# A fused attention and two-MLP kernel: the second head mix in calls of 128 keys, the scores in calls of up to 120 rows

## The chip, the cores and the metric

One core of a Trainium2 chip. The metric is the device time of one execution in microseconds (us); lower is better. The kernel before takes 1315.55 us, the median of three runs (1312.03 to 1316.77).

## The reference

Talking-heads attention feeds a gated MLP, and that a second MLP. All is float32; batch 4, 12 heads, 448 rows and keys, head size 64.

```python
scores = scale * np.matmul(q, k.transpose(0, 1, 3, 2))
scores = np.einsum('bhij,hg->bgij', scores, w_pre)        # first mix over heads
scores = scores - np.max(scores, axis=-1, keepdims=True)
attn = np.exp(scores)
attn = attn / (np.sum(attn, axis=-1, keepdims=True) + 1e-09)
attn = np.einsum('bhij,hg->bgij', attn, w_post)           # second mix over heads
x = np.matmul(attn, v)                                    # then 1792 x 768
x = (1 / (1 + np.exp(-(x @ w_gate))) * (x @ w_val)) @ w_out   # 768 -> 1536 -> 768
h = np.maximum(x @ w_in, 0.0)                             # 768 -> 2048
out = h * h @ w_out2
```

## The kernel before

Attention comes first, then the two MLPs. The query rows of a batch are cut into tiles of 60 to 120 rows, 17 tiles in all. A tile is cut into groups of 10 rows, and two groups make a duo; there are 90 duos. An iteration of the main loop puts out, in program order, the work of several duos at several stages. On TensorE the order within an iteration is: the first mix of duo t (`premix`), the scores of a later tile for one pair of heads when the list `front` says so (`scores`), the second mix of a duo three iterations back (`postmix`), and every few iterations a product with the values (`values`).

- `scores` (L190 to L220) takes one pair of heads of one tile. For each head of the pair (`o`), 64 rows of the array hold the head's q and 448 keys stream through. Up to 64 query rows are taken per call (the loop over `c0`, L203), so a tile of 100 rows takes two calls, of 64 and 36 columns. ScalarE copies both PSUM banks to SBUF (`e`, L214), and a DMA on SP's queue scatters them into `g` (L217), with heads and rows of a group together on the partitions.
- `premix` (L225) multiplies `g` by a block-diagonal matrix `wp` in four calls on 64 rows and 64 columns of the array each (L232), into `ps_m`. VectorE takes the maximum (L244), ScalarE the exponential (L251), VectorE the reciprocal of the sum (L259, L260), and GpSimd scales the second mix's weights by it (`wn`, L264).
- `postmix` (L273) has the exponentials `a` as the stationary operand: 60 rows (5 query rows by 12 heads) by a run of 64 keys. It streams the 60 columns of `wn`. A duo has two groups (`y`), two halves of the array's rows (`u`) and seven runs of 64 keys, so 28 calls (L289), each in a quarter of the array: `u` picks the rows and `o` the columns. The result stands with the keys on the partitions, in two PSUM banks; VectorE copies them to `ap` (L317).
- `values` (L327) multiplies `ap` by `v` over four blocks of 128 keys; 448 keys are three and a half blocks, and `v` is padded with zeros. Its calls use 128 rows and 64 columns of the array (L336).
- The four banks `bank` are lent in turn to scores, second mix and values by `room` (L394). They are cleared once at the start (L127), since the last half block of the second mix is never written.

In the innermost part of `postmix` a call's place in the array is set by the partitions it reads and writes:

```python
for o in range(min(2, -(-(S - jt * P) // HP))):
    j = min(jt * P + o * HP, S - HP)
    nc.tensor.matmul(ps[u][o * HP : (o + 1) * HP, y, jt], lhsT=x[r, j : j + HP], ...)
```

Beside this, `feed` puts out work for the MLPs as a planner with fixed costs says (`Feed`, L517): during attention it rearranges the weights (ScalarE L787 and L790, VectorE, GpSimd L807, DMAs on SP's queue), and after it the MLPs' 4284 matmuls (L917) follow in order. It steps by a fixed model time per iteration.

A float32 matmul call shows as two records in the trace, each with a weight load of its own (PEld). 2520 calls at L289 are 5040 records.

Of the kernel before, what the change touches and what calls it, by code (L numbers as in the profile page):

```python
# [19 lines left out]
P = 128  # L20
# [8 lines left out]
HP = P // 2  # L29
# [35 lines left out]
def attention(tc, feed, q, k, v, w_pre, w_post, xs, B, H, S, D):  # L65
# [10 lines left out]
    nc = tc.nc  # L76
# [24 lines left out]
    with ExitStack() as ctx, ExitStack() as mid, ExitStack() as left:  # L101
# [21 lines left out]
        g_of = [pg.tile([P, GT, S], F32, name=f"g{m}") for m in range(GB)]  # L123

        bank = [ps_b.tile([P, 4 * P], F32, name=f"ps_b{m}") for m in range(4)]
        for x in bank:
            nc.vector.memset(x, 0.0)  # L127

        def masks():
            nc.gpsimd.memset(wr, 0.0)  # L130
# [42 lines left out]
        k_t, q_t = {}, {}  # L173
# [16 lines left out]
        def scores(n, p):  # L190

            b, i0, rows = tiles[n]
            isz = full[n]
            if p == 0:
                g_t[n] = g_of[n % GB]
            kt = k_t.pop((b, p)) if i0 + rows == S else k_t[b, p]
            if n == 0 and p // 2 == 1:
                ps = [ps_m.tile([P, S], F32, tag="m", name="ps_s") for _ in range(2)]
            else:
                ps = [x[:, :S] for x in room(2)]  # L200
            for o in range(2):
                r = slice(o * D, (o + 1) * D)
                for c0 in range(0, isz, HP):  # L203
                    c = slice(c0, min(c0 + HP, isz))
                    nc.tensor.matmul(  # L205
                        ps[o][c], lhsT=q_t[n][r, p, c], rhs=kt[r], start=True, stop=True
                    )
            t = p4.tile([IM, 2, S], F32, tag="e", name="e")
            e = [t[:, o] for o in range(2)]
            for o in range(2):  # L210
                if o and n == 0:
                    nc.vector.tensor_copy(e[o][:isz], ps[o][:isz])
                else:
                    nc.scalar.copy(e[o][:isz], ps[o][:isz])  # L214
                to = g_t[n][G0 : G0 + GI * H].rearrange("(r h) g j -> h r g j", h=H)
                queue = nc.scalar if n == 0 and o else nc.sync
                queue.dma_start(  # L217
                    out=to[2 * p + o, :, : isz // GI],
                    in_=e[o][:isz],
                )  # L220
# [52 lines left out]
        def postmix(d):  # L273
            n, r0 = groups[duos[d][0]][:2]
            if r0 == 0:
                ap[n] = pp.tile([P, JT, H, IM], F32, tag="ap", name="ap")
            a, wn = a_t.pop(d)
            at = room(2)
            ps = [
                x[:, : 2 * JT * KH].rearrange("p (y t h r) -> p y t h r", y=2, t=JT, r=HB) for x in at  # L280
            ]

            for y, x in enumerate(a):
                for jt in range(JT):
                    for u in range(2):
                        r = slice(u * HP, u * HP + KH)
                        for o in range(min(2, -(-(S - jt * P) // HP))):
                            j = min(jt * P + o * HP, S - HP)
                            nc.tensor.matmul(  # L289
                                ps[u][o * HP : (o + 1) * HP, y, jt],  # L290
                                lhsT=x[r, j : j + HP],
                                rhs=wn[r, y].rearrange("p g i -> p (g i)"),
                                start=True,
                                stop=True,
                            )
            for u in range(2):
                pending.append((mixed, d, u, ps[u], at[u]))

# [81 lines left out]
        def next_scores():  # L380

            _, n, p = front.popleft()
            scores(n, p)
            if tiles[n][1] + tiles[n][2] == S:
                freed[0] += 1
            if p == (EARLY if n == 1 else 0) and n + 1 < NT:
                q_load(n + 1)
# [6 lines left out]
        def room(n):  # L394
            at = [bank.pop(0) for _ in range(n)]
            bank.extend(at)
            if any(x[-1] is y for x in pending for y in at):
                flush()
            return at
# [7 lines left out]
        for p in range(NP):  # L407
            scores(0, p)
        mixers()
        for _ in range(EARLY):  # L410
            scores(*front.popleft()[1:])
        for t in range(ND + 30):
# [18 lines left out]
            while done < ND and (done <= t - LAG or t >= ND and done <= t - 2):  # L431
                r0 = groups[duos[done][0]][1]
                n = groups[duos[done][0]][0]
                while r0 == 0 and todo and todo[0][1] <= n - 2:
                    values(*todo.popleft()[1:])
                    left_over -= VW
                postmix(done)
                left_over -= PW
                done += 1
                if done == ND or groups[duos[done][0]][0] != n:  # L440
                    todo.extend((t, n, h) for h in range(H // HV))
                if done == ND:
                    flush()
                    mid.close()
                    feed.widen(1)
# [714 lines left out]
@with_exitstack  # L1160
def whole(ctx, tc, q, k, v, w_pre, w_post, wg, wv, wo, wi2, wo2, out):
    B, H, S, D = k.shape[0], 2 * k.shape[1], k.shape[3], k.shape[2] // 2
    DM = out.shape[0]
    dram = ctx.enter_context(tc.tile_pool(name="dram", bufs=1, space=DRAM))
    xs = [dram.tile([DM, S], F32, name=f"xs{b}") for b in range(B)]
    with tc.manual_schedule():
        feed = mlp(ctx, tc, xs, wg, wv, wo, wi2, wo2, out)
        attention(tc, feed, q, k, v, w_pre, w_post, xs, B, H, S, D)
        feed.finish()
# [49 lines left out]
```

## Time and profile before

| | |
|---|---|
| median of three runs | 1315.55 us |
| profiled execution: time | 1321.79 us |
| profiled execution: span, first to last instruction | 1320.0 us |
| TensorE (PE) busy | 1233.4 us, 93% |
| weight loads (PEld) busy | 1062.1 us, 80% |
| VectorE / ScalarE / GpSimd busy | 77% / 61% / 23% |
| attention ends, MLP matmuls without a break begin | about 445 us |
| TensorE's granted clock, mean | 0.98 |

The profile gives each engine's busy time, the idle time before each group of instructions and what ended it. A record of a matmul lasts from its start to the modelled end of its pipeline, so records overlap, and the busy time of a group is the union of its records. "60*64 60x60" means a stationary operand of 60 rows by 64 columns, and 60 columns streamed.

### The profile page before, as it was taken

How to read it: one execution, taken by the hardware profiler on the slowest of the kernel's cores; microseconds unless marked ns; L12 is line 12 of the kernel's file. 1: busy time of each engine (PE TensorE's matmuls, PEld its weight loads, DVE VectorE, ACT ScalarE, POOL GpSimd, SP SyncE). 2: the span in 40 equal slices, each digit the busy share in tenths (PEclk: the TensorE clock that was granted, in tenths of full speed). 3: DMA queues.
4: the chain of work that ended last, by engine and by line, in shares of the span. 5: the costliest groups of instructions: out<-in, count | busy, mean ns of one | idle time of the engine just before them, and what ended most of it. 6: DMA issues, size and time to landing. Idle time of an engine off the chain costs nothing.

```text
span 1320.0 us, 32039 instructions
## 1 busy us (share of the span) xinstructions
PE 1233.4 (93%) x12476; PEld 1062.1 (80%) x12476; DVE 1020.6 (77%) x1681; ACT 805.5 (61%) x1545; POOL 307.8 (23%) x361
## 2 busy tenths in 40 slices
PE   5888978978887999999999999999999999999998
PEld 2556656655665999999999999998988999999998
DVE  3667667757776888899988789998899986566864
ACT  4676756756656756676666667665555675435553
POOL 5223333323332053420034343022342000000000
PEclk8999999989999999999999999999999999999999
DMA  5888888778787579874698887368686355334343
GB/s 171 227 222 239 232 247 238 230 235 236 224 242 252 158 261 313 294 259 133 201 311 287 295 297 224 115 217 313 207 281 212 108 179 170 108 108 110 108 130 108
DMA packets 151507, 280.50 MB, mean 213 GB/s; under 512 B 32892, under 2 KB 100796, under 8 KB 151356
## 3 DMA queue, kind: packets, MB, share of 16 engines
q1 hardware_dynamic: 150676, 277.81, 69.0%
q8 instruction: 98, 1.61, 0.5%
q10 hardware_dynamic: 680, 0.66, 0.2%
q14 instruction: 53, 0.43, 0.1%
HBM read 175.53 MB, written 63.31 MB: 181 GB/s over the span
## 4 chain that ended last, share of the span: by engine, by line
PE 74%; DMA 13%; DVE 6%; issue 3%; ACT 2%; SPq 0%; POOL 0%; ACTq 0%; DVEq 0%
PE ps L917 60%; DMA g<-e 4%; PE ps_b L336 4%; PE ps_b L289 4%; PE ps_m L232 3%; PE ps_b L205 3%; DMA raw<-in_wv 2%; DMA raw<-in_wo 2%; DMA raw<-in_wg 1%; DMA q<-in_q 1%; ACT a L251 1%; DVE ap L317 1%; DVE w L905 1%; DVE y L823 1%; DMA gv<-y 1%
## 5 line engine op out<-in xcount | busy, mean ns | idle before, releaser
L917 PE MATMUL ps<-s,w 128*128 128x448 f32 x4284 | 873.1, 366 | 7.6 <-DVE w L905 5.4
L917 PEld LDWEIGHTS ps<-s,w 128*128 128x128 f32 x4284 | 806.7, 188 | 73.9 <-DVE w L905 7.2
L905 DVE TENSOR_TENSOR w<-w,w 128x768 fp32r<-128x768 f32 x238 | 245.4, 1031 | 103.4 <-ACT w L902 101.5
L902 ACT CAST w<-w 128x768 fp32r<-128x768 f32 x238 | 199.1, 837 | 161.6 <-PE ps L917 135.1
L807 POOL TENSOR_TENSOR y<-y,raw 128x384 int32<-128x384 int32 x136 | 174.9, 1305 | 421.0 <-DVE y L796 177.4
L289 PEld LDWEIGHTS ps_b<-wn,a 60*64 60x64 f32 x5040 | 114.9, 138 | 54.8 <-issue 31.2
L317 DVE COPY ap<-ps_b 128x480 f32<-128x480 f32 (+2 forms) x177 | 108.3, 652 | 58.9 <-PE ps_b L289 58.7
L244 DVE TENSOR_REDUCE nm<-ps_m 128x1 f32<-128x448 f32 x180 | 103.4, 614 | 54.0 <-PE ps_m L232 53.9
L902 ACT CAST s<-g 128x448 fp32r<-128x448 f32 x196 | 109.8, 566 | 46.9 <-PE ps L917 38.8
L289 PE MATMUL ps_b<-wn,a 60*64 60x60 f32 x5040 | 119.9, 226 | 18.6 <-issue 11.5
L214 ACT COPY e<-ps_b 120x448 f32<-120x448 f32 (+2 forms) x196 | 95.0, 544 | 66.8 <-PE ps_b L205 48.7
L264 POOL TENSOR_SCALAR wn<-wq,sm 128x60 f32<-128x60 f32 x167 | 70.1, 435 | 261.7 <-DVE sm L260 198.0
L205 PE MATMUL ps_b<-k,q 64*64 64x448 f32 (+3 forms) x784 | 111.4, 578 | 19.2 <-DMA q<-in_q 8.7
L232 PE MATMUL ps_m<-g,wp 64*64 64x448 f32 (+1 forms) x720 | 104.9, 587 | 24.5 <-DMA g<-e 13.8
L905 DVE TENSOR_TENSOR s<-g,s 128x448 fp32r<-128x448 f32 x196 | 121.3, 633 | 3.2 <-ACT s L902 0.6
L251 ACT ACTIVATE a<-ps_m,nm 128x448 f32<-128x448 f32 x180 | 114.3, 648 | 13.6 <-PE ps_b L289 6.9
L336 PEld LDWEIGHTS ps_b<-ap,vraw 128*64 128x64 f32 x1632 | 76.8, 139 | 25.3 <-ACT e L214 14.5
L336 PE MATMUL ps_b<-ap,vraw 128*64 128x100 f32 (+4 forms) x1632 | 84.8, 261 | 12.9 <-ACT e L214 11.5
L205 PEld LDWEIGHTS ps_b<-k,q 64*64 64x64 f32 (+3 forms) x784 | 45.1, 135 | 61.8 <-issue 39.2
L787 ACT ACTIVATE raw<-raw 128x768 f32<-128x768 f32 x68 | 62.4, 918 | 39.7 <-DMA raw<-in_wo 11.0
L950 ACT COPY ps<-ps 128x448 f32<-128x448 f32 x104 | 52.0, 515 | 28.8 <-PE ps L917 28.1
L942 DVE TENSOR_TENSOR c<-ps,c 128x448 f32<-128x448 f32 x104 | 63.2, 619 | 7.7 <-PE ps L917 6.9
(49 smaller groups left out, 804.4 us busy)
## 6 DMA issues: line engine op xcount, KB each, us to landing
w<-wo SPq DMA_DIRECT2D x98, 384.0 KB
w<-gv SPq DMA_DIRECT2D x84, 384.0 KB
g<-e SPq DMA_DIRECT2D x108, 210.0 KB
raw<-in_wo SPq DMA_DIRECT2D x56, 384.0 KB
w<-wi SPq DMA_DIRECT2D x56, 384.0 KB
wo<-y SPq DMA_DIRECT2D x42, 384.0 KB
g<-e SPq DMA_DIRECT2D x84, 175.0 KB
gv<-y SPq DMA_DIRECT2D x36, 384.0 KB
```

The lines of the kernel that those rows point to most:

```text
L205: nc.tensor.matmul(ps[o][c], lhsT=q_t[n][r, p, c], rhs=kt[r], start=True, stop=True)
L214: nc.scalar.copy(e[o][:isz], ps[o][:isz])
L232: nc.tensor.matmul(ps[u * HP : (u + 1) * HP], lhsT=wp[r], rhs=g_t[n][r, 2 * t + u], start=True, stop=True,)
L244: nc.vector.tensor_reduce(out=nm[-1], in_=ps, op=ALU.max, axis=AX.X, negate=True)
L251: nc.scalar.activation(a, ps, AF.Exp, bias=nm, accum_out=sm[:, y : y + 1])
L289: nc.tensor.matmul(ps[u][o * HP : (o + 1) * HP, y, jt], lhsT=x[r, j : j + HP], rhs=wn[r, y].rearrange("p g i -> p (g i)"), start=True, sto ...
L317: nc.vector.tensor_copy(o, i)
L336: nc.tensor.matmul(ps[o * D : (o + 1) * D, e, :w], lhsT=vraw[b, h][:, x, jt, :], rhs=ap[n][:, jt, h * HV + x, :w], start=jt == 0, stop=jt ...
L807: e.tensor_tensor(out=y3, in0=y3, in1=word(0)[:, i].bitcast(I32), op=ALU.add)
L902: e.copy(dst.tile[:, 0], src.tile)
L905: e.tensor_tensor(out=dst.tile[:, 1], in0=src.tile, in1=dst.tile[:, 0].bitcast(F32), op=ALU.subtract)
L917: e.matmul(bank.tile, lhsT=a[k], rhs=x[l], start=start and n == 0, stop=stop and n == 2, skip_group_check=not fresh,)
```

## The change

The second mix takes runs of 128 keys: one call covers 60 rows of the array and all 128 columns. The fourth run starts at key 320, so that it overlaps the third (256 to 383) by 64 keys. A duo takes 16 calls in place of 28. The duplicated keys meet rows of zeros in `v`, which the host now inserts at 384 to 447 of the padded order, ahead of the last 64 keys. All 128 partitions are written, so the four clears of the banks go. The scores of a head take one call of the tile's whole height, up to 120 columns.

```diff
         bank = [ps_b.tile([P, 4 * P], F32, name=f"ps_b{m}") for m in range(4)]
-        for x in bank:
-            nc.vector.memset(x, 0.0)
...
             for o in range(2):
                 r = slice(o * D, (o + 1) * D)
-                for c0 in range(0, isz, HP):
-                    c = slice(c0, min(c0 + HP, isz))
-                    nc.tensor.matmul(
-                        ps[o][c], lhsT=q_t[n][r, p, c], rhs=kt[r], start=True, stop=True
-                    )
+                nc.tensor.matmul(
+                    ps[o][:isz], lhsT=q_t[n][r, p, :isz], rhs=kt[r], start=True, stop=True
+                )
...
                 for jt in range(JT):
+                    j = min(jt * P, S - P)
                     for u in range(2):
                         r = slice(u * HP, u * HP + KH)
-                        for o in range(min(2, -(-(S - jt * P) // HP))):
-                            j = min(jt * P + o * HP, S - HP)
-                            nc.tensor.matmul(
-                                ps[u][o * HP : (o + 1) * HP, y, jt],
-                                lhsT=x[r, j : j + HP],
...
+                        nc.tensor.matmul(
+                            ps[u][:, y, jt],
+                            lhsT=x[r, j : j + P],
...
-    vp = np.pad(v, ((0, 0), (0, 0), (0, -S % P), (0, 0)))
+    last = S - S % P
+    vp = np.insert(v, [last] * (-S % P), 0, axis=2)
```

On TensorE, an iteration in which two groups of a tile of 100 rows get a first mix, a score call's pair of heads, a values call and a second mix. Names with numbers are the four lent banks; the sizes are those written, partitions by columns. Before, from the first mix to the end of the first group's second mix:

```order
L232 MATMUL ps_m<-g_133,wp 64x448 x4
L205 MATMUL ps_b_136<-k,q 64x448
L205 MATMUL ps_b_136<-k,q 36x448
L205 MATMUL ps_b_137<-k,q 64x448
L205 MATMUL ps_b_137<-k,q 36x448
L336 MATMUL ps_b_134<-ap,vraw 64x60 x16
L289 MATMUL ps_b_135<-wn,a 64x60 x2
L289 MATMUL ps_b_136<-wn,a 64x60 x2
```

The last two rows stand three times, then once without the x2, and all that once more for the second group: 28 calls. The same place in the changed program:

```order
L228 MATMUL ps_m<-g_133,wp 64x448 x4
L201 MATMUL ps_b_136<-k,q 100x448
L201 MATMUL ps_b_137<-k,q 100x448
L331 MATMUL ps_b_134<-ap,vraw 64x60 x16
L284 MATMUL ps_b_135<-wn,a 128x60
L284 MATMUL ps_b_136<-wn,a 128x60
```

The last two rows stand eight times: 16 calls. Nothing has moved against anything else; calls became fewer and wider. Over the attention, the shape of the array's part (64 by 64, 64 by 128, 128 by 64) changes between neighbouring calls 73 times before and 236 times now, since the first mix keeps 64 by 64 while scores (but for the first tile, of 60 rows) and second mix have 64 by 128.

At the start of VectorE's queue, before and now:

```order
L127 MEMSET ps_b_134 128x512
L127 MEMSET ps_b_135 128x512
L127 MEMSET ps_b_136 128x512
L127 MEMSET ps_b_137 128x512
L212 COPY e<-ps_b_135 60x448
```

```order
L208 COPY e<-ps_b_135 60x448
L208 COPY e<-ps_b_137 60x448
```

The four clears are gone; the queues of ScalarE, GpSimd and SP have the same work in the same order.

## Rows read from the trace of the kernel before

**Rows 1.** The page: TensorE's busy tenths and granted clock in 40 slices of the span.

```profile
PE   5888978978887999999999999999999999999998
...
PEclk8999999989999999999999999999999999999999
```

**Rows 2.** Busy time by stretch: us, PE, PEld, DVE, ACT, POOL (instructions), clock, DMA, GB/s.

```profile
34.00:445.00 411.00, 349.15 (x8123) 255.90 (x8116) 285.46 (x630) 266.23 (x667) 122.70 (x218) 0.96 0.82 231
133.00:175.00 42.00, 39.60 (x936) 28.02 (x936) 30.71 (x71) 32.88 (x82) 15.21 (x27) 0.96 0.85 237
206.00:240.00 34.00, 31.85 (x744) 23.00 (x745) 24.60 (x58) 26.50 (x68) 12.02 (x22) 1.00 0.82 237
...
600.00:700.00 100.00, 100.00 (x495) 92.67 (x494) 88.70 (x133) 66.99 (x112) 19.28 (x13) 1.00 0.70 221
```

**Rows 3.** Groups of TensorE instructions, 34 to 445 us: busy us, mean ns, idle before.

```profile
L289 PE MATMUL ps_b<-wn,a 60*64 60x60 f32 x5040 | 119.9, 226 | 18.6 <-issue 11.5 <-POOL wn L264 4.3 <-DVE ap L317 1.8
L232 PE MATMUL ps_m<-g,wp 64*64 64x448 f32 x354 | 95.0, 585 | 24.0 <-DMA g<-e 13.8 <-ACT a L251 4.2 <-DMA q<-in_q 2.8
```

**Rows 4.** Timeline of TensorE, four single stretches: the longest waits of an iteration.

```profile
196.51 1.77 PE L232 MATMUL ps_m<-g,wp 64*64 64x448 f32 x8 [5.76 <-DMA g<-e]
...
273.36 1.40 PE L232 MATMUL ps_m<-g,wp 64*64 64x448 f32 x8 [4.14 <-DMA g<-e]
...
284.23 2.07 PE L336 MATMUL ps_b<-ap,vraw 128*64 128x120 f32 x18 [4.13 <-ACT e L214]
```

**Rows 5.** Timeline of TensorE: values calls of 60, 88, 108 and 120 streamed columns.

```profile
47.18 1.15 PE L336 MATMUL ps_b<-ap,vraw 128*64 128x60 f32 x32
...
152.91 1.43 PE L336 MATMUL ps_b<-ap,vraw 128*64 128x88 f32 x32
...
252.72 1.70 PE L336 MATMUL ps_b<-ap,vraw 128*64 128x108 f32 x32
...
210.96 1.86 PE L336 MATMUL ps_b<-ap,vraw 128*64 128x120 f32 x32 [0.90 <-ACT e L214]
```

**Rows 6.** Weight loads by form, 206 to 240 us (first three), 700 to 800 us (last).

```profile
L205 PEld LDWEIGHTS ps_b<-k,q 64*64 64x64 f32 x33 | 2.8, 133 | 2.1 <-issue 1.3 <-ACT e L214 0.5 <-ACT raw L790 0.2
L205 PEld LDWEIGHTS ps_b<-k,q 64*56 64x56 f32 x28 | 2.1, 127 | 0.8 <-issue 0.5
...
L205 PEld LDWEIGHTS ps_b<-k,q 64*36 64x36 f32 x4 | 0.3, 108 | 0.4 <-issue 0.4
...
L917 PEld LDWEIGHTS ps<-s,w 128*128 128x128 f32 x494 | 92.8, 188 | 7.3
```

**Rows 7.** Timeline of TensorE: second mixes, at full clock and (second row) at half.

```profile
310.98 1.21 PE L289 MATMUL ps_b<-wn,a 60*64 60x60 f32 x56
...
199.52 1.80 PE L289 MATMUL ps_b<-wn,a 60*64 60x60 f32 x53
...
148.97 1.03 PE L289 MATMUL ps_b<-wn,a 60*64 60x60 f32 x53
```

**Rows 8.** Timeline of TensorE: neighbours of different shape, 83 to 86 us.

```profile
83.09 1.14 PE L289 MATMUL ps_b<-wn,a 60*64 60x60 f32 x52 [0.17 <-DVE ap L317]
84.16 1.59 PE L336 MATMUL ps_b<-ap,vraw 128*64 128x100 f32 x32
85.68 0.98 PE L232 MATMUL ps_m<-g,wp 64*64 64x448 f32 x8
```

**Rows 9.** Timeline of TensorE: neighbours of the same shape, 147 to 149 us.

```profile
147.45 0.98 PE L232 MATMUL ps_m<-g,wp 64*64 64x448 f32 x8
148.22 0.96 PE L205 MATMUL ps_b<-k,q 64*64 64x448 f32 x8
```

**Rows 10.** Timeline of VectorE and TensorE at the program's start.

```profile
0.98 2.11 DVE L127 MEMSET ps_b<- 128x512 f32 x4 [0.98 <-PEq L1206]
...
4.68 3.12 PE L205 MATMUL ps_b<-k,q 64*60 64x448 f32 x8 [4.68 <-DMA k<-in_k]
```

More of the change, by code (lines that the diff above doesn't have):

```diff
@@ L284, in postmix @@
                 for jt in range(JT):
+                    j = min(jt * P, S - P)
                     for u in range(2):
                         r = slice(u * HP, u * HP + KH)
-                        for o in range(min(2, -(-(S - jt * P) // HP))):
-                            j = min(jt * P + o * HP, S - HP)
-                            nc.tensor.matmul(
-                                ps[u][o * HP : (o + 1) * HP, y, jt],
-                                lhsT=x[r, j : j + HP],
[L292 to L295, printed above, removed]
+                        nc.tensor.matmul(
+                            ps[u][:, y, jt],
+                            lhsT=x[r, j : j + P],
+                            rhs=wn[r, y].rearrange("p g i -> p (g i)"),
+                            start=True,
+                            stop=True,
+                        )
             for u in range(2):
```

## The prediction

> **What bounds the kernel now.** I read the page's slices first [rows 1]. From the fourteenth slice (33 us each) TensorE is at 9 tenths nearly throughout, and the slices of attention before it, up to about 445 us, show 5 to 9, most of them 7 or 8. The windows give the numbers [rows 2]: from 34 to 445 us TensorE is busy 349 us of 411, in the MLPs 100 of 100. So after attention the time is TensorE's own work, which the change leaves alone: a later start of the MLPs is a later end, one for one, and what matters is by how much the change moves the end of attention.
>
> There, TensorE is idle 62 us of 411. The long waits are for the scatter of scores through DMA and for ScalarE [rows 3, 4]: 5.76, 4.14 and 4.13 us are the three longest. In stretches without such a wait TensorE is busy 39.60 us of 42 and 31.85 of 34 [rows 2], which is 94%. VectorE has 285 us of work in the stretch and ScalarE 266, so neither is the bound. The second mix is the largest single customer of TensorE, 120 us in 5040 records [rows 3], two records to a call.
>
> **What one record of the second mix costs.** The values calls show what a record takes by the columns streamed [rows 5]. 32 records go to two parts of the array, 16 to each, one after the other. They take 1.43 us at 88 columns, 1.70 at 108 and 1.86 at 120: from 88 to 120 that is 0.43 us for 32 columns, 13.4 ns a column, 0.84 ns per column and record. On that line 60 columns would take 1.43 - 28 x 0.0134 = 1.05 us. The row says 1.15. Something other than streaming holds records of 60 columns, by 6 ns each. The weight load is the candidate: load records last 108 ns at 36 columns, 127 at 56, 133 at 64 and 188 at 128 [rows 6], so 0.86 ns a column (80 ns over 92 columns). 64 columns load in 55 ns where 60 stream in 50. With a few ns on top that is the step found: (1.15 - 0.22)/16 = 58 ns, 0.22 being one record's length.
>
> The second mix's own row agrees: its busiest quarter of the array takes 16 records (2 groups x 4 runs of keys x 2), 16 x 58 ns + 0.23 for the last = 1.16 us, and a whole one stands at 1.21 us [rows 7]. At half clock 53 records take 1.80 us where they take 1.03 at full clock [rows 7]; the step follows the array's clock and is no matter of issuing instructions.
>
> **The change, part by part.**
>
> *Second mix.* The calls go from 28 to 16 a duo, but the number of records that follow each other in one part of the array stays: before, the busiest quarter had 16, now each half of the rows has 2 groups x 4 runs x 2 = 16. Each now loads 128 columns in place of 64. The load, already the longer of the two, grows by 64 x 0.86 = 55 ns, so the step goes from 58 to 113 ns while streaming stays at 50. Per duo 16 x 55 ns = 0.88 us; 90 duos give **+79 us** of TensorE time. No row shows a load of 60 rows and 128 columns, nor two of them at once on the two halves. The bounds of the price: nothing, if wide loads go beside the streaming better than I think (streaming alone would then set 50 to 58 ns), and below nothing only if the number of records counted, which is a rival below; above, load and streaming one after the other, 113 + 50 = 163 ns, 16 x 105 ns x 90 = 151 us. I take 55 ns, because the nearest row, the one of 60 columns [rows 5], is a load-bound step and the load row of 128 columns [rows 6] scales as the others do.
>
> The trace shows loads running beside the streaming of the same quarter: 55 + 50 ns would not fit in 58. The Trainium skill, "TensorE: Matmul & The Clock Gate", Part 3, The mechanism, says that a load overlaps running matmuls only where the row group differs. By that rule the step would be the upper bound; the trace of 64-column parts disagrees with it, and no run here shows it for 128 columns.
>
> *Changes of shape.* From 73 to 236, 163 more. Where the shape changes, the next call starts 0.07 us before the end of the last (84.16 against 83.09 + 1.14; 85.68 against 84.16 + 1.59) [rows 8]. Where it stays, it starts 0.21 us before (148.22 against 147.45 + 0.98) [rows 9]. So a change costs 0.14 us, **+23 us** in all. The bounds: zero, if 64 by 64 and 64 by 128 count as one shape; and 0.2 us (33 us), as the first load of 128 columns is then exposed for 55 ns more. The row shows it for 64 by 64 against 128 by 64 alone. The Trainium skill, "TensorEngine Tiling (Array Packing)", Key Properties, says that any change of tiling mode drains the engine; by it the pair here pays too, and without it the sum would be 24 us less.
>
> *Scores.* 396 calls become 204. The four quarters worked at once, now two halves do, each with the same two records of 448 columns (448 x 0.84 = 376 ns). The load of 100 to 120 columns takes 86 to 103 ns under the streaming of 376. Zero; what covers it is the streaming itself, which does not go away. The copies and scatters behind it are the same.
>
> *The clears.* 2.11 us of VectorE from 0.98 us; TensorE's first call comes at 4.68 us and waits for a load of k [rows 10]. Zero. The order of `v` is the host's. Zero. VectorE copies the same 480 columns a bank, now all of them written.
>
> *Who waits.* A second mix lasts 0.9 us longer, so VectorE's copy to `ap`, the lent banks and the next calls come later; all of it is in order behind TensorE, and every iteration gets longer by the same time, which gives ScalarE, GpSimd and the DMAs more of it.
>
> **The sum.** 79 + 23 = 102 us more for TensorE in a stretch where it is busy 349 of 411. If all 62 us of idle took up work, attention would end 40 us later; if none did, 102. I take the share that TensorE reaches where no long wait stands, 94%: (349 + 102)/0.94 = 480, so **+69 us**. I take off 4 us for the clock: it is 0.96 in this stretch and 1.00 where TensorE does not wait [rows 2], and waits get fewer; 2% of 451 us of work is 9 us, and I count half. That makes +65. The profiled execution took 1321.8 us, 6.2 above the median of 1315.55. Its time would be 1387; on the median of the runs I forecast **1380**.
>
> **The rivals.**
>
> - *The wide load is hidden* (chance 0.09). Then only the changes of shape cost, 0 to 23 us, most of it in the idle time: (349 + 23)/0.94 = 396 is under the 411 there are now. 1316 to 1332. For it: two wide loads may share what four narrow ones had. Against: loads of 128 columns take 55 ns more [rows 6].
> - *Load and streaming in turn* (chance 0.07), the rule above: 151 + 23 = 174, (349 + 174)/0.94 = 556, +145: about 1460. Against: the 58 ns step of now.
> - *Fewer records, faster* (chance 0.06). If TensorE's queue, not the array, set the pace of the second mix, its 32 records in place of 56 would count. 56 take 1.21 - 0.23 = 0.98 us, 17.5 ns each; 24 fewer save 0.42 us a duo, 38 us. It decides if it is more than the changes of shape cost, thus if these cost less than 0.23 us each; at 0.14 it leaves -15 us, 1301. For it: TensorE's waits before the second mix are put down to "issue" for 11.5 us [rows 3]. Against: at half clock the same records take 1.75 times as long.
> - *Nothing is moved* (chance 0.03): the added work is real but fits wholly into the waits for DMA and ScalarE. Between 1309 and 1322.
>
> **How the numbers follow.** The forecast has 0.75, and its own range is 1355 to 1418 (idle filled or kept, +40 to +102). In it lie about 0.68 of all cases. To reach 8 in 10 the range goes down to 1318, over most of the first rival, and up to 1425. What a measurement of this kernel can tell from no change is about 0.5%, 6.6 us. Faster by more than that: the third rival, 0.06. Within it: a part of the first, and the last, 0.06. Slower: 0.88.
>
> **What would show it.** In the profile after: weight loads of 64 rows by 128 columns with about 185 ns each; a whole second mix of 32 records at 2.0 to 2.1 us in place of 1.21; the first mix starting some 0.07 us before the end of what stands ahead of it, where it was 0.15 to 0.2; TensorE busy over 94% from 34 us to the end of attention, with waits for the scatter shorter; that end at 500 to 515 us; the MLPs as long as now. Wrong: second mixes of 1.2 us or less with wide loads (the first rival or the third), of 2.8 us (the second), or second mixes of 2 us with the end of attention where it was (the last).

## The result, and the profile after

The change makes the kernel slower by 1.4%: the median of four runs is 1333.1 us (1327.96 to 1337.19) against 1315.2 for the kernel before, a ratio of 1.0137 with an interval of 1.0095 to 1.0179. The forecast was 1380 us, slower by 65 us; the direction held and the size did not, 18 us in place of 65. 1333 lies inside the wide range of 1318 to 1425, but at its low end, which was there for a wide load that is hidden; as the rows below show, the load is not hidden, so that part of the range was right by luck.

| | before | after |
|---|---|---|
| median of the runs, us | 1315.2 | 1333.1 |
| profiled execution: time / span, us | 1321.8 / 1320.0 | 1334.7 / 1332.9 |
| first MLP matmul (end of attention), us | 433.8 | 444.6 |
| from there to the end of the span, us | 886.2 | 888.3 |
| TensorE busy from 34 us to that point, us | 338 of 399.8 | 408 of 410.6 |

The profiled execution of the kernel before is one of its slower ones, 6.6 us above its median where that of the changed kernel is 1.6 above its own, so the two profiles show some 5 us less of a difference than the medians. In the profiles 10.8 of the 12.9 us between the spans lie in attention. The page of the changed kernel, TensorE's tenths and granted clock in 40 slices, against [rows 1]:

```profile
PE   6999999999999999999999999999999999999998
...
PEclk9999999999999999999999999999999999999999
```

The windows of both kernels from 34 us to the first MLP matmul, the kernel before first (us, then busy us and instructions of PE, PEld, DVE, ACT, POOL, then clock, DMA share, GB/s):

```profile
34.00:433.80 399.80, 337.95 (x8068) 245.52 (x8060) 277.08 (x616) 258.08 (x650) 122.70 (x218) 0.96 0.82 233
```

```profile
34.00:444.60 410.60, 408.24 (x5553) 295.73 (x5549) 277.98 (x616) 263.16 (x647) 122.41 (x218) 1.00 0.76 226
```

TensorE was idle 62 us of 400 and is now idle 2.4 of 411. The waits for the scatter and for ScalarE [rows 4] are gone, and the mean clock of the stretch went from 0.96 to 1.00. VectorE, ScalarE and GpSimd did the same work in a slightly longer time.

The timeline of TensorE in the changed kernel, two iterations without and one with a values call, shows the priced parts, against [rows 5, 7 to 9]:

```profile
207.29 0.98 PE L228 MATMUL ps_m<-g,wp 64*64 64x448 f32 x8
208.21 1.02 PE L201 MATMUL ps_b<-k,q 64*120 64x448 f32 x4
209.06 1.90 PE L284 MATMUL ps_b<-wn,a 60*128 60x60 f32 x32
210.88 0.98 PE L228 MATMUL ps_m<-g,wp 64*64 64x448 f32 x8
211.79 1.02 PE L201 MATMUL ps_b<-k,q 64*120 64x448 f32 x4
212.65 1.90 PE L284 MATMUL ps_b<-wn,a 60*128 60x60 f32 x32
214.47 1.86 PE L331 MATMUL ps_b<-ap,vraw 128*64 128x120 f32 x32
```

and its weight loads, 200 to 300 us, against [rows 6]:

```profile
L284 PEld LDWEIGHTS ps_b<-wn,a 60*128 60x128 f32 x690 | 43.0, 188 | 7.2 <-issue 5.1 <-POOL wn L260 0.7 <-POOL y L802 0.4
L331 PEld LDWEIGHTS ps_b<-ap,vraw 128*64 128x64 f32 x360 | 17.2, 137 | 2.9 <-DVE nm L240 2.0 <-ACT e L210 0.7
```

A second mix takes 1.90 us. Records of the same half of the array start 112 ns after each other (111 or 112 in 2293 of 2700 pairs), and the load record of 128 columns lasts 188 ns. From one first mix to the next it is 210.88 - 207.29 = 3.59 us, and TensorE is never idle in between. Where the shape changes, the next call starts just before the end of the last: L201 at 208.21 against 207.29 + 0.98, L228 at 210.88 against 209.06 + 1.90. Where it stays, it starts 0.17 us before (L284 at 209.06 against 208.21 + 1.02).

### The profile page after: what moved, and what is told of

The parts are those of the page before. It is cut to its first block, busy times and chain, and to the rows that moved or that the text cites. A ratio compares the mean times of both kernels' runs of the same rounds, so it can differ in the third digit from the quotient of the medians.

```text
span 1332.9 us, 26911 instructions
## 1 busy us (share of the span) xinstructions
PE 1307.3 (98%) x9932; PEld 1107.8 (83%) x9932; DVE 1022.5 (77%) x1677; ACT 812.4 (61%) x1545; POOL 305.8 (23%) x361
## 4 chain that ended last, share of the span: by engine, by line
PE 90%; DVE 4%; DMA 2%; issue 1%; ACT 1%; POOL 0%; SPq 0%; ACTq 0%; DVEq 0%
PE ps L912 59%; PE ps_b L284 12%; PE ps_b L201 6%; PE ps_m L228 6%; PE ps_b L331 6%; DVE w L900 1%; DMA raw<-in_wo 1%; DVE y L818 1%; DMA w<-wi 1%; DVE s L900 0%; DVE g L1106 0%; DVE c L937 0%; DMA q<-in_q 0%; DVE y L788 0%; DMA vraw<-in_v 0%
## 5 line engine op out<-in xcount | busy, mean ns | idle before, releaser
L284 PEld LDWEIGHTS ps_b<-wn,a 60*128 60x128 f32 x2880 | 177.3, 188 | 34.5 <-issue 26.6
L312 DVE COPY ap<-ps_b 128x480 f32<-128x480 f32 (+2 forms) x177 | 109.1, 656 | 100.0 <-PE ps_b L284 99.4
L284 PE MATMUL ps_b<-wn,a 60*128 60x60 f32 x2880 | 176.8, 271 | 0.9 <-ACT e L210 0.8
L201 PE MATMUL ps_b<-k,q 64*120 64x448 f32 (+2 forms) x400 | 103.7, 599 | 11.6 <-DMA q<-in_q 6.8
L201 PEld LDWEIGHTS ps_b<-k,q 64*120 64x120 f32 (+2 forms) x400 | 30.1, 175 | 81.1 <-ACT a L247 39.7
L228 PE MATMUL ps_m<-g,wp 64*64 64x448 f32 x720 | 92.1, 569 | 1.9 <-DVE wq L163 1.0
L331 PEld LDWEIGHTS ps_b<-ap,vraw 128*64 128x64 f32 x1632 | 74.9, 137 | 12.1 <-DVE nm L240 6.6
```

The lines of the kernel that those rows point to most:

```text
L201: nc.tensor.matmul(ps[o][:isz], lhsT=q_t[n][r, p, :isz], rhs=kt[r], start=True, stop=True)
L228: nc.tensor.matmul(ps[u * HP : (u + 1) * HP], lhsT=wp[r], rhs=g_t[n][r, 2 * t + u], start=True, stop=True,)
L284: nc.tensor.matmul(ps[u][:, y, jt], lhsT=x[r, j : j + P], rhs=wn[r, y].rearrange("p g i -> p (g i)"), start=True, stop=True,)
L312: nc.vector.tensor_copy(o, i)
L331: nc.tensor.matmul(ps[o * D : (o + 1) * D, e, :w], lhsT=vraw[b, h][:, x, jt, :], rhs=ap[n][:, jt, h * HV + x, :w], start=jt == 0, stop=jt ...
```

## The experiments

Two theories were tried first. *Share theory*, the forecast's step: busy time is work, and TensorE reaches 94% of a stretch. *Work theory*: at full rate TensorE's work before was 90 iterations of 2.34 us, about 81 us of values calls and 10 of changes of shape, 302 us of 400; the added work goes into the free 98 us first. Its 2.34 us is from a first mix of the kernel before at 147.45 [rows 9] to the next, in the timeline:

```profile
149.79 0.59 PE L232 MATMUL ps_m<-g,wp 64*64 64x448 f32 x1
```

From run 5 on a third was tried, *supply theory*: TensorE's instruction stream, which comes in packets of some 255 (the last section), sets the pace. Ratios are to the kernel before on the same chip, with 95% intervals.

**Run 1: the second mix alone.** The change without its scores:

```diff
-                nc.tensor.matmul(
-                    ps[o][:isz], lhsT=q_t[n][r, p, :isz], ...
+                for c0 in range(0, isz, HP):
+                    c = slice(c0, min(c0 + HP, isz))
+                    nc.tensor.matmul(ps[o][c], lhsT=q_t[n][r, p, c], ...
```

> The second mix of the change with the scores of before. In the profile of the changed kernel an iteration without values calls takes TensorE 3.59 us (207.29 to 210.88) where before it took 2.34 (147.45 to 149.79); the second mix has 1.0 of the 1.25 us. Work theory: TensorE's own work in attention before was 90 x 2.34 = 211 us, about 81 us of values calls and 10 of changes of shape, 302 us in a stretch of 400, so that nearly 100 us were free although only 62 showed as idle; added work fills them first. Here 302 + 79 + some 20 for changes of shape = 401: the end of attention moves by 0 to 8 us, time 1315 to 1324, TensorE's idle time in attention under 10 us. Share theory (the forecast's step: busy time is work, and 6% stays idle): (349 + 99)/0.94 = 477, 1370 to 1385.

Measured 1330.3 us, ratio 1.0138 (1.0091 to 1.0184); attention ends at 441.7 us with 3.8 us idle. The work theory's stretch (0 to 8 us later) holds, though the time passed the 1315 to 1324 it gave; the share theory's (1370 to 1385) does not. The second mix carries the change; the scores add nothing that the intervals separate.

**Runs 2 to 4: the kernel before with more of its second mix.** The loop runs again over the first group, over both, or twice more over both:

```diff
-            for y, x in enumerate(a):
+            for y, x in [(0, a[0]), *enumerate(a)]:   # run 2
+            for y, x in [*enumerate(a)] * 2:          # run 3; * 3 in run 4
```

> The kernel before, with the first group's second mix of each duo issued twice into the same place, same result: a dose of TensorE work with no wide load and no change of shape. 8 records of 58 ns more in the busiest quarter, 0.46 us x 90 = 42 us. Work theory: 302 + 42 = 344 of 400, no change, 1309 to 1320; idle time falls. Share theory: (349 + 42)/0.94 = 416 against 411 now, 1318 to 1330.

> The kernel before with the whole second mix issued twice: 16 records more in a row, 0.93 us x 90 = 84 us, nearly the dose of the change without its shapes. Work theory: 302 + 84 = 386 of 400, 1312 to 1322. Share theory: (349 + 84)/0.94 = 461, +50, 1355 to 1375. If the change is cheap for another reason (say, because wide calls spare the queue), this kernel must be clearly slower than the changed one (1333).

> The kernel before with the second mix issued three times: 167 us more of TensorE work. Work theory: 302 + 167 = 469, past the free time, so the end of attention moves by 65 to 75 us, 1380 to 1392, idle near zero. Share theory: (349 + 167)/0.94 = 549, +138, 1445 to 1465.

Measured: 1.0268 (1.0182 to 1.0353), 1.0785 (1.0737 to 1.0833) and 1.1796 (1.1688 to 1.1904): 36, 103 and 242 us by the medians. Both theories fell: 84 us of array time cost 103 where the work theory allowed 10 and the share theory 50. TensorE's groups in run 3, 34 to 530 us, show what is new:

```profile
L289 PE MATMUL ps_b<-wn,a 60*64 60x60 f32 x10080 | 212.3, 225 | 46.4 <-issue 45.5 <-DVE ap L317 0.2
```

45.5 us of idle time before the second mix are put down to "issue", which the profile uses where no other engine or DMA was waited for. Narrow calls are thus no clean dose: a second mix before is 112 instructions (56 records, each with a load) and 58 ns x 16 of array time. The next runs took work and instructions apart.

**Runs 5 and 6: work with few instructions.** The first mix, 16 instructions and 0.75 us, issued twice and three times:

```diff
-            for y, ps in enumerate(a_t[d]):
+            for y, ps in [*enumerate(a_t[d])] * 2:   # * 3 in run 6
```

> The kernel before with the first mix of each duo issued twice into the same place, same result: 8 records of 448 columns in four quarters, 0.75 us a duo, 68 us of TensorE work in all, with 16 instructions a duo (the second mix has 112) and no change of shape. Doubling the second mix cost 103 us, more than its 84 us of array time, with 45 us of TensorE waits put down to issue; this dose has the work and hardly the instructions. Work theory (302 us of work at full rate in a stretch of 400, added work fills the free time first): 302 + 68 = 370, 0 to +12 us, 1311 to 1325. Share theory (the forecast's step): (349 + 68)/0.94 = 444 against 411, +33, 1340 to 1355. Supply theory (what a stretch costs is set by TensorE's instruction stream, fetched 256 at a time; 1440 more of some 16,400): as the work theory here.

> The same with the first mix three times: 136 us more. Work theory: 302 + 136 = 438 of 400, so +38 to +48 us, 1350 to 1362, and TensorE idle under 10 us in attention. Share theory: (349 + 136)/0.94 = 516, +105, 1410 to 1425.

Measured 1.0142 (1.0085 to 1.0198) and 1.0473 (1.0418 to 1.0529), 16 and 61 us by the medians. Both lie some 4 to 13 us above the work theory and far below the share theory (33 and 105). The windows from 34 us to the first MLP matmul, run 5 and run 6:

```profile
34.00:430.30 396.30, 380.12 (x8740) 271.99 (x8736) 279.59 (x614) 256.41 (x646) 122.67 (x218) 1.00 0.79 234
```

```profile
34.00:477.90 443.90, 440.04 (x9447) 304.49 (x9439) 280.19 (x616) 257.15 (x648) 122.55 (x218) 1.00 0.71 210
```

With 68 us more work attention ends no later than before (430.3 against 433.8); with 136 it ends 44 us later and TensorE is full, 440.0 us of 443.9. So the work at full rate before was 440 - 136 = 304 us, as the iterations had it, and not 338 or 349; the 136 is an estimate, two more first mixes of 0.75 us in each of 90 duos. In run 5 the rest of the program took 893 us against 886; the cause of that stays open.

**Run 7: instructions with little work.** 28 calls ahead of each second mix:

```diff
+            for y, x in enumerate(a):
+                for i in range(14):
+                    u, o = i % 2, i // 2 % 2
+                    r = slice(u * HP, u * HP + KH)
+                    nc.tensor.matmul(ps[u][o * HP : o * HP + 33, y, 0, 0, :1],
+                                     lhsT=x[r, :33], rhs=wn[r, y, 0, :1], ...)
```

> The kernel before with 28 small calls ahead of each second mix, 33 columns loaded and one streamed, into places that the mix overwrites; shape 64 by 64, so no change of shape. Array time 14 records x 33 us/1000 = 0.46 us a duo, 42 us in all, what issuing half the second mix twice adds (that cost 36 us), but 112 instructions a duo in place of 56. Supply theory: what doubling the second mix costs, it costs by its instructions: here +80 to +110 us, 1390 to 1420, waits put down to issue as there (45 us). Work theory: like the half dose or less, 1311 to 1350.

Measured 1.0826 (1.0758 to 1.0895), 107 us by the medians: what the whole second mix again costs, from half its array time (an estimate) and the same number of instructions. The window to the first MLP matmul, and TensorE's groups, 34 to 524 us:

```profile
34.00:524.70 490.70, 410.03 (x13101) 306.93 (x13093) 275.75 (x614) 262.90 (x646) 121.89 (x218) 0.92 0.64 191
```

```profile
L300 PE MATMUL ps_b<-wn,a 60*64 60x60 f32 x5040 | 122.7, 232 | 37.5 <-issue 37.5
...
L287 PE MATMUL ps_b<-wn,a 60*33 60x1 f32 x5040 | 75.4, 172 | 18.7 <-issue 17.4 <-DVE ap L328 0.3 <-POOL wn L264 0.3
```

The supply theory holds for the kernels with more calls; the last section has what the trace shows of it. Not all of the 107 us is waiting for instructions: the mean granted clock of the stretch is 0.92, against 0.96 before.

**Run 8: the scores alone**, with the second mix and the clears of before.

> The scores of the change with the second mix of before. 192 calls fewer (768 instructions of some 16,400), some 150 changes of shape more at 0.14 us = 21 us of TensorE work. Work theory: 302 + 21, no change, 1305 to 1318. Share theory: (349 + 21)/0.94 = 394 against 411, no change either. Supply theory: 3 fetches of 64 less, a small gain, 1300 to 1312.

Measured 1.0027 (0.9992 to 1.0061). No theory is told apart; the scores' part of the change costs at most 0.6%.

**Runs 9 and 10: fewer instructions and less load.** Run 9 loads 96 keys of 128, run 10 uses wide calls for the second group alone:

```diff
-                            ps[u][:, y, jt],
-                            lhsT=x[r, j : j + P],
+                            ps[u][:96, y, jt],              # run 9
+                            lhsT=x[r, j : j + 96],
```

```diff
+                        w = HP if y == 0 else P             # run 10
+                        for c in range(0, P, w):
+                            if jt * P + c < S - HP or c + w == P:
+                                nc.tensor.matmul(ps[u][c : c + w, y, jt], lhsT=x[r, j + c : j + c + w], ...
```

> The changed kernel with 96 of the 128 keys of each second-mix call: it leaves out the keys 96 to 127 of every run (places in the banks that hold older values take their part; the four clears are back). All calls, instructions and shapes stay; only the load is 32 columns shorter, 27 ns by 0.86 ns a column, so the step of a record goes from 112 to about 85 ns and a mix of 32 records from 1.90 to about 1.47 us. TensorE's work falls by 16 x 27 ns x 90 = 39 us, from 408 (changed kernel, 34 us to the end of attention, 2 us idle) to 369. What held the kernel before at 400 us while it had some 300 of work decides the rest: if waits that both kernels share hold it (scatters, ScalarE), the floor stays near 400 and the time comes to 1310 to 1322; if the instruction supply holds it (5088 of 16,352 instructions fewer here than before), the floor is lower and the time comes to 1290 to 1305.

> Second mix of a duo's first group in calls of 64 keys, of its second group in calls of 128; scores as before; same result. 22 calls a duo in place of 28 (2160 instructions fewer than before, 8 of 64 fetches), TensorE work 302 + 40 for the wide half + 20 for changes of shape = 362 of 400. Work theory with shared waits: 1308 to 1320. With the instruction supply as what holds the kernel before: 1290 to 1305, the best of both.

Measured 1.0036 (1.0004 to 1.0069) and 1.0021 (0.9988 to 1.0053). A second mix of run 9 on the timeline:

```profile
146.39 1.50 PE L286 MATMUL ps_b<-wn,a 60*96 60x60 f32 x32
```

1.50 us against 1.90, forecast 1.47: the price of the load per column is confirmed, 0.40 us for 32 columns and 16 records, 25 ns each. The time did not go below that of the kernel before, though both kernels have fewer instructions than it, 78 and 90 packets in place of 98, and none of TensorE's waits in their attention is put down to issue. The window of run 9 to the first MLP matmul says how far this goes:

```profile
34.00:428.30 394.30, 385.15 (x5553) 266.38 (x5549) 277.60 (x616) 256.53 (x650) 122.90 (x218) 0.96 0.80 236
```

TensorE is busy 385 of 394 us here (381 of 394 in run 10): with more work than the kernel before, these two could end attention at most 9 and 13 us earlier unless their records got shorter. So they don't settle whether the supply holds the kernel before; run 12, with its very TensorE instructions, does.

**Run 11: scores earlier.**

```diff
-AHEAD = 3
+AHEAD = 5
```

> The kernel before with the scores of the next tile placed up to two iterations earlier (AHEAD 5 in place of 3), so that the scatter into g has two iterations more (about 9 us) before the first mix reads it; instructions and work the same. If late scatters (the longest waits before: 5.76, 4.14 us, 13.8 in all) set the length of attention, these waits go and the time falls by 8 to 20 us, 1290 to 1303. If the instruction supply sets it, no change, 1303 to 1316.

Measured 1.0035 (0.9997 to 1.0073). Late scatters do not set it: TensorE's waits for `g` fall from 13.8 to 5.3 us and those for the exponential from ScalarE rise from 4.2 to 8.5 us, and the time does not fall. Where TensorE waits less for one thing it waits for the next.

**Runs 12 and 13: less rearrangement of weights beside attention**, in the kernel before and in the changed one:

```diff
-                feed.step(4.0)
+                feed.step(2.5)
```

> The kernel before with the planner stepped by 2.5 in place of 4.0 model microseconds per iteration of attention, so that about a third of the weight rearrangement done beside attention (loads and stores by DMA, ScalarE L787 and L790, VectorE, GpSimd) is put out after it; all the work is done, same result. The runs so far end attention (first MLP matmul) at 423 to 434 us whether TensorE's instructions are fewer (8, 9, 10) or the scores earlier (11). If the rearrangement, which shares DMA, ScalarE and VectorE, holds that floor: attention ends at 390 to 415 us, TensorE idle in it below 50; the MLPs may take longer by what was put off (time 1280 to 1320). If the order of attention's own steps holds it: attention ends at 420 to 434 us still, time 1305 to 1330.

> The changed kernel with the planner at 2.5 as in run 12. There the kernel before ended attention at 393 us in place of 434. If TensorE's own work (408 us from 34 us on, 2.5 us idle) alone holds the changed kernel, its attention ends at 438 to 446 us as without this edit (444.6), 45 to 50 us behind run 12, with TensorE idle under 6 us; the MLPs wait for their first weights less than in run 12. If the rearrangement holds it too, attention ends at 405 to 430 us.

Measured 1.0154 (1.0091 to 1.0216) and 1.0528 (1.046 to 1.0597). The windows to the first MLP matmul, run 12 and run 13:

```profile
34.00:393.20 359.20, 328.66 (x8056) 241.55 (x8048) 253.00 (x586) 243.24 (x631) 97.60 (x193) 0.97 0.78 226
```

```profile
34.00:440.80 406.80, 404.77 (x5548) 294.43 (x5544) 255.67 (x586) 251.38 (x629) 97.23 (x193) 1.00 0.68 199
```

The kernel before ends attention 41 us earlier, the changed one 4 us; both as the theory of a rearrangement that holds the kernel before, and TensorE the changed one, had it. This is the clearest pair of the study: with the same lighter load on the other engines and the DMAs, the change costs 440.8 - 393.2 = 47.6 us of attention, where at 4.0 it costs 10.8. The sum of work agrees with both: 112 us more meet 359.2 - 302 = 57 free us in run 12, which leaves 55, and 399.8 - 302 = 98 at 4.0, which leaves 14. Run 12 has the instructions of the kernel before, so their supply does not hold that kernel's attention at 434 us. Both then take some 45 us longer for the rest (932 us in either, against 886 and 888), which run 12's range (1280 to 1320) had not allowed for, and run 13 was expected to wait less. What is lost there is not at the MLPs' start: in either run TensorE works for some 155 us and then waits for weights `w` from ScalarE, here the longest wait of run 12 and of run 13:

```profile
584.86 1.11 PE L917 MATMUL ps<-s,w 128*128 128x448 f32 x2 [25.53 <-ACT w L902]
```

```profile
632.45 1.12 PE L912 MATMUL ps<-s,w 128*128 128x448 f32 x2 [25.42 <-ACT w L897]
```

**Runs 14 and 15: the planner at 3.4 and 3.7** in the kernel before.

> The kernel before with the planner at 3.4: between 4.0 (attention ends at 434, nothing late in the MLPs) and 2.5 (393, but 46 us lost in the MLPs' start). If the rearrangement beside attention holds the end of attention in proportion, it ends near 415 to 422 us; if its weights are in time, the time is 1293 to 1303, below both kernels; if not, 1305 to 1320.

> As run 14 with the planner at 3.7. In proportion attention ends near 424 to 430 us; time 1300 to 1308 if its weights are in time.

Measured 1.0145 (1.01 to 1.019) and 1.011 (1.0076 to 1.0145); both took about 1328.6 us, above all that was expected. In the profiles attention ends at 407.5 and 407.4 us, and the rest takes 927 and 905 us against 886; these two executions took 1336.2 and 1314.9 us, so neither figure for the rest is that of a median execution. The end of attention does not follow the planner's step in proportion (415 to 422 and 424 to 430 were expected), and what it gains is lost in the wait for late weights. No kernel of the study beats the one before.

## Why the prediction was wrong, point by point

- *The price of the wide load* was right: step 113 ns forecast and 111 to 112 found, a load record of 188 ns for about 185, and run 9 gives 25 ns for 32 columns where 0.86 ns a column makes 27. 2.0 to 2.1 us were forecast for a second mix; it takes 1.90.
- *The changes of shape* were right: L228 behind L284 starts 0.08 us before its end, where the old borders had 0.07 [rows 8], and L284 behind L201, same shape, 0.17. Iteration for iteration, 3.59 - 2.34 = 1.25 us times 90 is 112 us of added work; the sum had 102.
- *Scores and clears* were right at zero (runs 1 and 8; the first matmul waits for k as before).
- *The step that failed is the sum*, (349 + 102)/0.94. First, 349 was not work. 11 of it belong to the MLPs, whose matmuls began at 433.8 and not 445 us (338 of 399.8). Of the 338, only about 302 are work at full rate: run 6 gives 304, the changed kernel 408 - 112 = 296. Up to 16 us of the difference is half-rate clock (a mean of 0.96 between the two levels, 2.4 and 1.2 GHz, is 8% of 400 us at the lower). The other 20 us were not measured; a part is the modelled ends of records that run on into a wait (by an estimate 12 us: about 60 waits, 0.2 us each). The 4 us taken off for the clock were thus too few: the stretch after has a mean of 1.00. Second, the 94% were read as what TensorE can reach; it reached 99.4%, since most of its waits came from a pace that other work set and vanished when its own became the slower. With 302 + 112 = 414 us and no waits the end of attention comes out at 34 + 414 = 448 us; measured are 408 us and 444.6.
- *What set the pace before* I had not named. I wrote that VectorE at 285 us and ScalarE at 266 were not the bound and took TensorE for it. Attention ends at 423 to 434 us in the kernel before and in runs 5 and 8 to 11, with more work on TensorE, with fewer instructions or with earlier scores. Runs 12, 14 and 15 lower that to 393 and 407 us by putting off weight rearrangement, with TensorE's instructions as before. That the rearrangement holds it there is shown. What keeps another 57 us free in run 12 (359.2 - 302) stays open, and by which of its parts (DMA share 0.82, ScalarE, VectorE, GpSimd, or their order in the queues) the rearrangement acts was not tried.
- *The rivals.* The one nearest to the result had 0.03: the added work real, but inside the waits. It was right in the mechanism, but for the last 10.8 us (18 by the medians); the room was not the 62 us of visible waits but some 98. "Fewer records, faster" is half right in its cause: the supply of instructions is a cost on this engine (run 7), but not what bound the kernel before (run 12; some 17 of its 62 us of idle are put down to issue). The wide load is not hidden, and not in turn with streaming either: in turn, the step would be 163 ns, and the trace has 112. The Trainium skill, "TensorE: Matmul & The Clock Gate", Part 3, The mechanism, has the sentence that a load overlaps running matmuls only where the row group differs; the trace disagrees, for 128 columns now too, but the same section also lets a load into a background weight buffer be pulled ahead, which would fit. The Trainium skill, "TensorEngine Tiling (Array Packing)", Key Properties, says that changing the tiling mode drains the engine; the trace agrees as far as the overlap of neighbours shrinks from 0.17 to some 0.07 us.

## What to carry to other kernels

Busy time of TensorE is not its work: before adding to it, take the shortest clean iteration from the timeline, multiply, and compare with the stretch. What is left over was nearly free here (68 us more cost 16 in run 5), though the engine read 338 us busy of 400, as long as the added work came in few instructions: in many it cost more than its array time (runs 3 and 7). A second mix of fewer, wider calls pays for its load columns, not for its count, once the load is longer than the streaming. And if a stretch is paced by work put beside it, an engine's added work there costs what passes the free time; that a saving on the engine would be worth nothing there follows from the same reasoning, but no run here took work off TensorE below that of the kernel before.

## What the runs showed of the hardware that was not expected

TensorE's instructions arrive in packets, and where many short ones follow each other it waits for the next packet: now and then in the kernel before, often in run 7. The page's queue 8, before, changed, and run 7:

```profile
q8 instruction: 98, 1.61, 0.5%
```

```profile
q8 instruction: 78, 1.28, 0.4%
```

```profile
q8 instruction: 138, 2.26, 0.7%
```

98 packets for 2 x 12476 matmuls and loads are 255 instructions each. Run 7 has 40 packets more, 42 us of array time more (an estimate), 107 us more time, and 79 us of TensorE's idle time in attention put down to "issue" (37.5, 17.4, 12.1, 6.8 and 4.8 us by group), where the kernel before has some 17; run 5, with 68 us of array time and 6 packets more, has 13. The packed trace has the packets' times, and they show that the waits are for them: with TensorE's instructions numbered in the order of their starts, each of the 60 waits of over 0.15 us put down to issue in run 7's attention, and each of the 19 in that of the kernel before, stands ahead of an instruction whose number is 193 or 194 above a multiple of 256, and ends 1.2 to 1.8 us after a packet of queue 8 has ended. The Trainium skill, "Runtime: NRT & Kernel Launch", Instruction fetch mechanics, has blocks of 256 instructions, which agrees, and calls the cost of crossing into the next mostly hidden, which run 7 does not bear out. The DMAs' mean share in run 7's attention is 0.64; whether the packets are late because of them was not tried.
